# Reading an up-projection's result once: the clamp at minus one on VectorE, and the rest from SBUF

## The chip, the cores and the metric

The kernel runs on one core of a Trainium2 chip. The core has five engines that work side by side, each through its own queue in order: TensorE (PE, with its weight loads listed as PEld), VectorE (DVE), ScalarE (ACT), GpSimd (POOL) and SyncE (SP), which here only issues transfers. Matmul results land in PSUM, which the kernel uses as eight banks of 128 x 512 float32; everything else lies in SBUF. The metric is the device time of one execution in microseconds, and the time of a kernel is the median of its timed runs.

## The reference

Two steps follow each other. The first is an attention without softmax, for 4 batches x 4 heads x 1088 tokens x 32 dimensions, with features that are outer products of two small projections; the second is a feed-forward layer on the 4352 tokens, with a 128 x 2048 matrix up and a 2048 x 128 matrix down:

```
phi(x) = outer(S1 x, S2 x)                    # 8 x 8 = 64 features
kv = sum_s phi(k) v ; z = sum_s phi(k)
x  = (phi(q) kv) / (phi(q) z + 1e-6)
h  = x @ w_in
g  = h                 where h >= 1
     0                 where h <= -1
     (h + 1)^2 / 4     between
out = g @ w_out
```

All inputs come in as float64 and are turned into float32 on the chip. The matmuls of the feed-forward layer run on numbers of a shorter form (fp32r); so that little precision is lost, each operand is split into a high and a low part, and three products are summed (high x high, low x high, high x low).

## The kernel before, in words

**The feed-forward layer** is cut into 144 units: 8 chunks of 512 tokens and one of 256, each with 16 slices of 128 of the 2048 hidden features. The list `units` (L248) gives their order; the first two chunks are woven into each other, and so are the last two. For a unit, `up` (L257) makes three matmuls into one bank, `h` (L262 to L264), and then the curve, whose result g is needed in two parts, `g_hi` and `g_lo = g - g_hi`:

- ScalarE reads the bank, `s = relu(0.5 h + 0.5)` (L270), and squares s in SBUF (L271). So s is ((h+1)/2)^2, and 0 below minus one.
- VectorE computes `min(max(h, 1), s)` from the bank and s. It does so once for g in full precision (L275), and for some 62% of the units a second time, rounded to the short form, for `g_hi` (L274). For the other units ScalarE makes `g_hi` as a cast of g (L277). The function `share` picks them by the fractions in `HI_ACT` (L25): half of the first 32 units, 35% of the rest.
- GpSimd subtracts, `g_lo = g - g_hi`, from SBUF (L278). For the last four units VectorE does it.

`down` (L282) then adds three matmuls into the chunk's accumulator bank, `acc` (L289 to L291). In the program's text it follows its unit by `LAG` = 4 units.

**The attention** is written as generators (`k_steps`, `q_steps`), from which the main loop takes a step after each unit, so that the features of a later batch are computed between units. VectorE has the outer products (L165), the division (L219 to L221) and part of the copies out of PSUM (L207, L235, L236) of that work.

**The weights** of the feed-forward layer are converted by `from_double` in pieces of 512 columns (L82 to L105): VectorE takes the words apart, from and to SBUF (L82, L87, L89, L91, L94), ScalarE has three operations and GpSimd three subtractions, products and sums (L102, L104, L105). Two pieces come before the first unit, the six others between the first units.

**What sets the order:** the program's text is not the order of execution. The context is opened with a scheduler (L412) that places the instructions of each engine by a simulated timeline; on the chip each engine's queue is then worked through in that order, with semaphores between the engines. All PSUM tiles come from one pool of eight banks, and a bank is reused when its last reader is done. SBUF tiles of the curve have rings: five for s and g, six for `g_hi` and `g_lo`.

Of the kernel before, what the change touches and what calls it, by code (L numbers as in the profile page):

```python
# [8 lines left out]
F32 = mybir.dt.float32  # L9
# [4 lines left out]
AF = mybir.ActivationFunctionType  # L14
ALU = mybir.AluOpType
PSUM = bass.MemoryType.PSUM

P = 128
# [2 lines left out]
HI_MAX = 0x47EFFFFF  # L21
HI_MIN = 0x38100000
LAG = 4
FIRST = 32
HI_ACT = (0.5, 0.35)  # L25
FS = "k k k 0f 1f 2f k 0t k 0t 1t 1t K 0n 1n K 0x 2t 2t 1x 2n 2x w"
SS = "0f k k 0t 0t 1f 0n k 1t 0x 1t 2f k 2t 1n 2t 2n 1x k 2x"

# [8 lines left out]
def tile_kernel(ctx: ExitStack, tc: tile.TileContext, qT, kT, v, S, w_in, w_out, outT):  # L37
    nc = tc.nc
# [7 lines left out]
    CH = 512  # L46
# [6 lines left out]
    el = ctx.enter_context(tc.tile_pool(name="el", bufs=3))  # L53
    ps = ctx.enter_context(tc.tile_pool(name="ps", bufs=8, space=PSUM))

    def bank(name):
        return ps.tile([P, 512], F32, tag="ps", name=name)
# [89 lines left out]
    def x_tiles(c0):  # L147
        if c0 not in x_of:
            x_of[c0] = [xs.tile([P, CH], F32R, tag=f"x_{w}", name=f"x_{w}{c0}") for w in ("hi", "lo")]
        return x_of[c0]  # L150
# [97 lines left out]
    units = [*woven(chunks[0], chunks[1], 2), *((c0, n, j) for c0, n in chunks[2:-2] for j in range(NJ)),  # L248
             *woven(chunks[-2], chunks[-1], 3)]

    def share(u, f):
        return int((u + 1) * f) > int(u * f)

    made = {}
    accs = {}

    def up(u):  # L257
        c0, n, j = units[u]
        x_hi, x_lo = x_tiles(c0)
        fj = slice(j * P, (j + 1) * P)  # L260
        h = bank(f"h{u}")
        nc.tensor.matmul(h[:, :n], lhsT=wi_hi[:, fj], rhs=x_hi[:, :n], start=True, stop=False)  # L262
        nc.tensor.matmul(h[:, :n], lhsT=wi_hi[:, fj], rhs=x_lo[:, :n], start=False, stop=False)  # L263
        nc.tensor.matmul(h[:, :n], lhsT=wi_lo[:, fj], rhs=x_hi[:, :n], start=False, stop=True)  # L264

        s = el.tile([P, CH], F32, tag="s", name=f"s{u}", bufs=5)
        g = el.tile([P, CH], F32, tag="g", name=f"g{u}", bufs=5)
        g_hi = el.tile([P, CH], F32R, tag="g_hi", name=f"g_hi{u}", bufs=LAG + 2)
        g_lo = el.tile([P, CH], F32R, tag="g_lo", name=f"g_lo{u}", bufs=LAG + 2)
        nc.scalar.activation(s[:, :n], h[:, :n], AF.Relu, bias=0.5, scale=0.5)  # L270
        nc.scalar.activation(s[:, :n], s[:, :n], AF.Square)  # L271
        by_act = share(u, HI_ACT[u >= FIRST])
        if not by_act:
            nc.vector.scalar_tensor_tensor(out=g_hi[:, :n], in0=h[:, :n], scalar=1.0, in1=s[:, :n], op0=ALU.max, op1=ALU.min)  # L274
        nc.vector.scalar_tensor_tensor(out=g[:, :n], in0=h[:, :n], scalar=1.0, in1=s[:, :n], op0=ALU.max, op1=ALU.min)  # L275
        if by_act:
            nc.scalar.copy(g_hi[:, :n], g[:, :n])  # L277
        (nc.vector if u >= len(units) - 4 else nc.gpsimd).tensor_tensor(  # L278
            out=g_lo[:, :n], in0=g[:, :n], in1=g_hi[:, :n].bitcast(F32), op=ALU.subtract)
        made[u] = (g_hi, g_lo)  # L280
# [63 lines left out]
    for u in range(len(units)):  # L344
        c0, n, j = units[u]
        while todo and todo[0][0] <= j:
            _, src, hi, lo, c, raws, tag = todo.pop(0)
            if c not in raws:
                raws[c] = load_weights(src, c, tag)
            make_weights(raws[c], hi, lo, c)  # L350
        while ready < c0 + n:
            advance()
        first_weights()
        up(u)
        advance()
        if u >= LAG:
            down(u - LAG)
# [58 lines left out]
```

## Time and profile before

| | |
|---|---|
| time, median of 3 runs | 282.25 us (281.66 to 283.06) |
| span of the profiled execution | 423.2 us |
| TensorE clock granted in the profiled execution | 0.555 of full speed |
| busy, PE / DVE / ACT / POOL in the profiled execution | 418.1 / 222.2 / 219.5 / 204.6 us |

The profiled execution is not one of the timed runs, and it lasted half as long again: all through it TensorE was granted little more than half of its clock. The span is the profiled execution's own time from its first to its last instruction; no other time of it is recorded. The durations of the other three engines are their own and do not follow TensorE's clock. So the page has to be read in two parts: how long an operation takes on VectorE, ScalarE and GpSimd can be taken over as it stands, while TensorE's durations, and with them what waits for what, have to be worked out again for a faster clock.

### The profile page before, as it was taken

To read this page: it belongs to the slowest core of one execution; us is meant where nothing else is said; L and a number is where in the kernel's file an instruction comes from. 1 tells how busy PE (TensorE), PEld (TensorE's weight loads), DVE (VectorE), ACT (ScalarE), POOL (GpSimd) and SP (SyncE) were. 2 spreads that over 40 slices of the span, in tenths; PEclk is the share of its full clock that TensorE was granted. 3 is DMA by queue.
4 is the path that set the end of the run, shared out by engine and by line. 5 is a ranking of instruction groups with operands and counts; after the bars stand their busy time and mean duration, and the time that the engine had idled before them with its cause. 6 is when DMAs were issued, how large, how long until landed. Compare 5 with 4: busy or idle time off the path is not lost.

```text
span 423.2 us, 4212 instructions
## 1 busy us (share of the span) xinstructions
PE 418.1 (99%) x1413; PEld 290.9 (69%) x1413; DVE 222.2 (53%) x390; ACT 219.5 (52%) x422; POOL 204.6 (48%) x173
## 2 busy tenths in 40 slices
PE   8999999999999999999999999999999999999997
PEld 6997877778766767786767655555555555567775
DVE  4469966566365453544563463554444444425543
ACT  2336646563354564433544466655566565556662
POOL 0046774747633424333343426646646546435751
PEclk6555555555555555555555555555555555555555
DMA  7942110010000010000000000000000000000001
GB/s 269 415 163 71 52 57 0 2 57 0 0 2 0 0 51 1 1 2 0 0 25 2 0 0 25 2 1 1 25 2 0 0 25 0 2 25 1 2 1 37
DMA packets 4629, 13.90 MB, mean 33 GB/s; under 512 B 512, under 2 KB 1152, under 8 KB 4608
## 3 DMA queue, kind: packets, MB, share of 16 engines
q1 hardware_dynamic: 4608, 13.64, 8.8%
q8 instruction: 11, 0.18, 0.2%
q14 instruction: 10, 0.08, 0.1%
HBM read 11.41 MB, written 2.23 MB: 32 GB/s over the span
## 4 chain that ended last, share of the span: by engine, by line
PE 97%; DMA 1%; DVE 0%; SPq 0%; ACT 0%; issue 0%; ACTq 0%
PE h L264 13%; PE h L262 13%; PE h L263 13%; PE acc L291 12%; PE acc L289 12%; PE acc L290 12%; PE kv L187 6%; PE nd L213 5%; PE tp L206 3%; PE ab_q L160 3%; PE ab_k L160 2%; PE xt L226 2%; DMA q_sb<-in_qT 1%; SPq L113 0%; DVE kp L165 0%; DVE topw L91 0%
## 5 line engine op out<-in xcount | busy, mean ns | idle before, releaser
L278 POOL TENSOR_TENSOR g_lo<-g,g_hi 128x512 fp32r<-128x512 f32 (+1 forms) x140 | 173.1, 1250 | 179.7 <-ACT g_hi L277 108.4
L270 ACT ACTIVATE s<-h 128x512 f32<-128x512 f32 (+1 forms) x144 | 82.3, 574 | 148.9 <-PE h L264 148.2
L274 DVE SCALAR_TENSOR_TENSOR g_hi<-h,s 128x512 fp32r<-128x512 f32 (+1 forms) x89 | 58.0, 651 | 95.5 <-ACT s L271 55.1
L275 DVE SCALAR_TENSOR_TENSOR g<-h,s 128x512 f32<-128x512 f32 (+1 forms) x144 | 92.8, 653 | 27.5 <-ACT s L271 26.7
L271 ACT ACTIVATE s<-s 128x512 f32<-128x512 f32 (+1 forms) x144 | 84.7, 605 | 1.3
L262 PE MATMUL h<-x_hi,wi_hi 128*128 128x512 f32 (+1 forms) x144 | 82.4, 572 | 0.4 <-ACT x_hi L235 0.4
L289 PE MATMUL acc<-g_hi,wo_lo 128*128 128x512 f32 (+1 forms) x144 | 81.4, 566 | 0.0
L264 PE MATMUL h<-x_hi,wi_lo 128*128 128x512 f32 (+1 forms) x144 | 80.6, 560 | 0.0
L291 PE MATMUL acc<-g_lo,wo_hi 128*128 128x512 f32 (+1 forms) x144 | 80.3, 565 | 0.0
L290 PE MATMUL acc<-g_hi,wo_hi 128*128 128x512 f32 (+1 forms) x144 | 79.5, 552 | 0.0
L263 PE MATMUL h<-x_lo,wi_hi 128*128 128x512 f32 (+1 forms) x144 | 79.5, 552 | 0.0
L290 PEld LDWEIGHTS acc<-g_hi,wo_hi 128*128 128x128 f32 x144 | 33.5, 232 | 17.4 <-issue 8.4
L289 PEld LDWEIGHTS acc<-g_hi,wo_lo 128*128 128x128 f32 x144 | 33.3, 231 | 17.3 <-issue 8.6
L291 PEld LDWEIGHTS acc<-g_lo,wo_hi 128*128 128x128 f32 x144 | 33.2, 232 | 16.7 <-issue 8.6
L264 PEld LDWEIGHTS h<-x_hi,wi_lo 128*128 128x128 f32 x144 | 31.2, 216 | 19.6 <-issue 12.0
L262 PEld LDWEIGHTS h<-x_hi,wi_hi 128*128 128x128 f32 x144 | 33.9, 236 | 15.5 <-issue 7.1
L263 PEld LDWEIGHTS h<-x_lo,wi_hi 128*128 128x128 f32 x144 | 32.9, 228 | 16.6 <-issue 10.4
L277 ACT CAST g_hi<-g 128x512 fp32r<-128x512 f32 (+1 forms) x55 | 32.8, 596 | 10.6 <-DVE g L275 10.6
L187 PEld LDWEIGHTS kv<-v_sb,kp 128*128 128x128 f32 x144 | 30.3, 298 | 2.4 <-issue 0.8
L213 PEld LDWEIGHTS nd<-kv_sb,qpT 128*128 128x128 f32 x144 | 29.1, 289 | 3.5 <-issue 1.5
L187 PE MATMUL kv<-v_sb,kp 128*128 128x66 f32 x144 | 29.1, 363 | 0.0
L213 PE MATMUL nd<-kv_sb,qpT 128*128 128x66 f32 x144 | 28.4, 348 | 0.0
(58 smaller groups left out, 267.8 us busy)
## 6 DMA issues: line engine op xcount, KB each, us to landing
v_sb<-in_v SPq DMA_DIRECT2D x4, 594.0 KB, 6.6
q_sb<-in_qT SPq DMA_DIRECT2D x4, 576.0 KB, 7.8
raw_i<-in_w_in SPq DMA_DIRECT2D x4, 512.0 KB, 8.5
raw_o<-in_w_out SPq DMA_DIRECT2D x4, 512.0 KB, 9.7
outT<-o SPq DMA_DIRECT2D x8, 256.0 KB, 2.0
k_sb<-in_kT SPq DMA_DIRECT2D x3, 576.0 KB, 9.3
k_sb<-in_kT SPq DMA_DIRECT2D x3, 192.0 KB, 2.5
outT<-o SPq DMA_DIRECT2D x1, 128.0 KB, 1.9
```

The lines of the kernel that those rows point to most:

```text
L187: nc.tensor.matmul(kv[:, p * VC : (p + 1) * VC], lhsT=kp[:, t, p * P : (p + 1) * P], rhs=v_sb[:, t, p * VC : (p + 1) * VC], start=(t == 0) ...
L213: nc.tensor.matmul(nd[:, c : c + VC], lhsT=qpT[:, p, i * P : (i + 1) * P], rhs=kv_sb[b][:, p].rearrange("p h c -> p (h c)"), start=True, s ...
L262: nc.tensor.matmul(h[:, :n], lhsT=wi_hi[:, fj], rhs=x_hi[:, :n], start=True, stop=False)
L263: nc.tensor.matmul(h[:, :n], lhsT=wi_hi[:, fj], rhs=x_lo[:, :n], start=False, stop=False)
L264: nc.tensor.matmul(h[:, :n], lhsT=wi_lo[:, fj], rhs=x_hi[:, :n], start=False, stop=True)
L270: nc.scalar.activation(s[:, :n], h[:, :n], AF.Relu, bias=0.5, scale=0.5)
L271: nc.scalar.activation(s[:, :n], s[:, :n], AF.Square)
L275: nc.vector.scalar_tensor_tensor(out=g[:, :n], in0=h[:, :n], scalar=1.0, in1=s[:, :n], op0=ALU.max, op1=ALU.min)
L278: (nc.vector if u >= len(units) - 4 else nc.gpsimd).tensor_tensor(out=g_lo[:, :n], in0=g[:, :n], in1=g_hi[:, :n].bitcast(F32), op=ALU.subt ...
L289: nc.tensor.matmul(acc[:, :n], lhsT=wo_lo[:, fj], rhs=g_hi[:, :n], start=(j == 0), stop=False)
L290: nc.tensor.matmul(acc[:, :n], lhsT=wo_hi[:, fj], rhs=g_hi[:, :n], start=False, stop=False)
L291: nc.tensor.matmul(acc[:, :n], lhsT=wo_hi[:, fj], rhs=g_lo[:, :n], start=False, stop=(j == NJ - 1))
```

## The change: what it does

The curve is computed by another chain, with the same value. VectorE clamps h at minus one, from the bank into a new SBUF tile `c` with a ring of four; this is the bank's only reader. ScalarE squares from `c`, with the scale and bias that stood in the Relu before (at c = -1 this gives 0). VectorE takes `min(max(c, 1), s)` with both inputs in SBUF, and the cast to `g_hi` is ScalarE's for every unit. The subtraction for `g_lo` stays where it was. So a unit goes from two ScalarE and one or two VectorE operations, with a third on ScalarE where VectorE has one, to two on each.

```diff
-FIRST = 32
-HI_ACT = (0.5, 0.35)
...
-    def share(u, f):
-        return int((u + 1) * f) > int(u * f)
...
-        nc.scalar.activation(s[:, :n], h[:, :n], AF.Relu, bias=0.5, scale=0.5)
-        nc.scalar.activation(s[:, :n], s[:, :n], AF.Square)
-        by_act = share(u, HI_ACT[u >= FIRST])
-        if not by_act:
-            nc.vector.scalar_tensor_tensor(out=g_hi[:, :n], in0=h[:, :n], scalar=1.0, in1=s[:, :n], op0=ALU.max, op1=ALU.min)
-        nc.vector.scalar_tensor_tensor(out=g[:, :n], in0=h[:, :n], scalar=1.0, in1=s[:, :n], op0=ALU.max, op1=ALU.min)
-        if by_act:
-            nc.scalar.copy(g_hi[:, :n], g[:, :n])
+        c = el.tile([P, CH], F32, tag="c", name=f"c{u}", bufs=4)
+        nc.vector.tensor_scalar(out=c[:, :n], in0=h[:, :n], scalar1=-1.0, scalar2=None, op0=ALU.max)
+        nc.scalar.activation(s[:, :n], c[:, :n], AF.Square, bias=0.5, scale=0.5)
+        nc.vector.scalar_tensor_tensor(out=g[:, :n], in0=c[:, :n], scalar=1.0, in1=s[:, :n], op0=ALU.max, op1=ALU.min)
+        nc.scalar.copy(g_hi[:, :n], g[:, :n])
         (nc.vector if u >= len(units) - 4 else nc.gpsimd).tensor_tensor(
             out=g_lo[:, :n], in0=g[:, :n], in1=g_hi[:, :n].bitcast(F32), op=ALU.subtract)
```

The scheduler makes a new order of it. Line numbers move up by up to eight: in the changed kernel L266 is the clamp, L267 the square, L268 g, L269 the cast and L270 `g_lo`.

**VectorE where the attention's work runs out** (units 78 to 82 of 144; a number behind a tile's name is only its place in the program, and h_2174 before and h_2252 after belong to unit 78). Before:

```order
L274 SCALAR_TENSOR_TENSOR g_hi_2180<-h_2174,s_2178 128x512
L275 SCALAR_TENSOR_TENSOR g_2179<-h_2174,s_2178 128x512
L275 SCALAR_TENSOR_TENSOR g_2195<-h_2190,s_2194 128x512
L274 SCALAR_TENSOR_TENSOR g_hi_2212<-h_2206,s_2210 128x512
L275 SCALAR_TENSOR_TENSOR g_2211<-h_2206,s_2210 128x512
L274 SCALAR_TENSOR_TENSOR g_hi_2228<-h_2222,s_2226 128x512
L275 SCALAR_TENSOR_TENSOR g_2227<-h_2222,s_2226 128x512
L275 SCALAR_TENSOR_TENSOR g_2243<-h_2238,s_2242 128x512
```

and in the changed kernel:

```order
L266 TENSOR_SCALAR c_2260<-h_2252 128x512
L268 SCALAR_TENSOR_TENSOR g_2223<-c_2226,s_2222 128x512
L266 TENSOR_SCALAR c_2277<-h_2269 128x512
L268 SCALAR_TENSOR_TENSOR g_2240<-c_2243,s_2239 128x512
L234 TENSOR_TENSOR x_lo_1936<-xt_2_1929,x_hi_1935 128x256
L266 TENSOR_SCALAR c_2294<-h_2286 128x512
L268 SCALAR_TENSOR_TENSOR g_2257<-c_2260,s_2256 128x512
L266 TENSOR_SCALAR c_2311<-h_2303 128x512
L268 SCALAR_TENSOR_TENSOR g_2274<-c_2277,s_2273 128x512
```

Each unit now has its clamp two units ahead of its g, the two in turn; no row of VectorE reads h and s together any more.

**ScalarE at the same place.** Before, with two rows for each unit and a cast for about one unit in three:

```order
L270 ACTIVATE s_2210<-h_2206 128x512
L277 CAST g_hi_2164<-g_2163 128x512
L270 ACTIVATE s_2226<-h_2222 128x512
L271 ACTIVATE s_2210<-s_2210 128x512
L271 ACTIVATE s_2226<-s_2226 128x512
```

and in the changed kernel:

```order
L267 ACTIVATE s_2256<-c_2260 128x512
L269 CAST g_hi_2224<-g_2223 128x512
L267 ACTIVATE s_2273<-c_2277 128x512
L269 CAST g_hi_2241<-g_2240 128x512
L267 ACTIVATE s_2290<-c_2294 128x512
L269 CAST g_hi_2258<-g_2257 128x512
```

ScalarE no longer reads h; it takes the square of one unit and the cast of the unit two before it in turn.

## The prediction, as it stood before the changed kernel was run

> **What bounds the kernel now.** I read the head of the page first, then the chain that ended last (its last row here is the one long piece of it that isn't TensorE's: start us, us):
>
> ```profile
> PE 418.1 (99%) x1413; PEld 290.9 (69%) x1413; DVE 222.2 (53%) x390; ACT 219.5 (52%) x422; POOL 204.6 (48%) x173
> PEclk6555555555555555555555555555555555555555
> PE 97%; DMA 1%; DVE 0%; SPq 0%; ACT 0%; issue 0%; ACTq 0%
> 2.60 6.00 DMA q_sb<-in_qT
> ```
>
> In the profiled execution TensorE is everything: 97% of the chain, at a granted clock of about 0.555. The timed runs took 282.25 us, against 423.2 us for this execution. Under the same clock that cannot be, since TensorE alone was busy for 418.1 us. At full clock its work would be 418.1 x 0.555 = 232 us, an estimate from these rows, and 282.25 us needs a mean clock of at least 232 / 282 = 0.82. The other engines' durations stay. So in the timed runs VectorE's 222, ScalarE's 220 and GpSimd's 205 us no longer vanish behind TensorE, and I ask stage by stage what is longest. I cut the span at 38 us (first unit's h), 115 us (end of the weight conversion) and 250 us (end of the attention); columns are the stretch, its length, and busy us with counts of PE, PEld, DVE, ACT, POOL:
>
> ```profile
> 0.00:38.00 38.00, 36.06 (x159) 32.01 (x159) 22.55 (x45) 13.32 (x30) 9.14 (x16) 0.56 0.64 240
> 38.00:115.00 77.00, 77.00 (x292) 59.26 (x290) 51.51 (x79) 41.58 (x81) 52.37 (x40) 0.55 0.10 31
> 115.00:250.00 135.00, 135.00 (x476) 95.08 (x476) 67.28 (x126) 64.23 (x117) 50.91 (x40) 0.56 0.02 6
> 250.00:423.00 173.00, 170.06 (x491) 104.57 (x489) 80.88 (x142) 100.39 (x195) 92.23 (x78) 0.56 0.02 9
> ```
>
> With PE's figures times 0.555, the longest engine is, in the second stretch, POOL with 52.4 us (PE 42.7, DVE 51.5); in the third PE with 74.9; in the fourth ACT with 100.4 (PE 94.4, POOL 92.2). The first is a wait for data and then TensorE work at low clock; I put it at 28 us, between 24 (about 9 us until the queries land, and half of the rest) and 38. Sum: 28 + 52.4 + 74.9 + 100.4 = 255.7 us. The time shown is 26.6 us above that floor, for hand-overs and for unevenness within a stretch. So with a fast TensorE no engine rules the whole, and each stretch has two or three within a tenth of each other.
>
> **The change part by part.** Durations by shape:
>
> ```profile
> L278 POOL TENSOR_TENSOR g_lo<-g,g_hi 128x512 fp32r<-128x512 f32 x128 | 164.8, 1299 | 174.6 <-ACT g_hi L277 103.3 <-DVE g L275 43.5 <-PE acc L291 16.0
> L275 DVE SCALAR_TENSOR_TENSOR g<-h,s 128x512 f32<-128x512 f32 x128 | 86.4, 683 | 27.1 <-ACT s L271 26.2 <-POOL g_lo L278 0.7
> L271 ACT ACTIVATE s<-s 128x512 f32<-128x512 f32 x128 | 79.1, 630 | 1.3
> L270 ACT ACTIVATE s<-h 128x512 f32<-128x512 f32 x128 | 76.3, 598 | 142.6 <-PE h L264 142.0
> L278 POOL TENSOR_TENSOR g_lo<-g,g_hi 128x256 fp32r<-128x256 f32 x12 | 8.8, 732 | 5.2 <-ACT g_hi L277 5.2
> L274 DVE SCALAR_TENSOR_TENSOR g_hi<-h,s 128x512 fp32r<-128x512 f32 x77 | 53.0, 688 | 93.8 <-ACT s L271 53.5 <-PE acc L290 27.1 <-ACT g_hi L277 5.4
> L277 ACT CAST g_hi<-g 128x512 fp32r<-128x512 f32 x51 | 31.2, 612 | 10.3 <-DVE g L275 10.3
> L82 DVE TENSOR_SCALAR hcw<-raw_o 128x512 f32<-128x512 f32 x4 | 1.7, 418 | 0.0
> L207 DVE COPY qpT<-tp 128x384 f32<-128x384 f32 x9 | 5.0, 558 | 16.7 <-PE tp L206 16.7
> L235 DVE CAST x_hi<-xt 128x256 fp32r<-128x256 f32 x1 | 0.4, 425 | 2.1 <-PE h L264 2.1
> ```
>
> *ScalarE* loses the Relu (0.60 us a unit) and casts the other 77 large units (0.61): per unit 0.63 + 0.61 = 1.24 us for 0.60 + 0.63 + 0.4 x 0.61 = 1.47. In the fourth stretch, where neighbours overlap by about a tenth (100.4 us of busy time), that is 74 units' worth (66 large, 16 small as half) x 0.23 x 0.9 = 15 us less: 85.
>
> *VectorE* gains a clamp for every unit. No row of before shows it; it is bounded by a one-input read of a bank, 0.558 us at 384 and 0.425 at 256 elements (so 0.69 at 512), and by the two-input 0.68 of L275; I take 0.68. Of it 0.62 counts, since neighbours start about 0.6 us apart (a row of the timeline below has two in 1.27). It loses such a read on 77 large units. The load per unit goes from 0.99 to 1.24 us. That alone is bearable. What the page's averages do not show is the second change: **g now has both inputs in SBUF**. Operations over the whole execution, min/median/max in ns:
>
> ```profile
> L274 DVE SCALAR_TENSOR_TENSOR g_hi<-h,s x89: 411/691/693, 43.1 to 415.8; 128x512 fp32r<-128x512 f32 x77, 128x256 fp32r<-128x256 f32 x12
> L275 DVE SCALAR_TENSOR_TENSOR g<-h,s x144: 412/680/694, 43.7 to 416.2; 128x512 f32<-128x512 f32 x128, 128x256 f32<-128x256 f32 x16
> L89 DVE SCALAR_TENSOR_TENSOR mw<-hcw,mw x8: 679/1086/1655, 13.8 to 101.5; 128x512 int32<-128x512 int32 x8
> L91 DVE SCALAR_TENSOR_TENSOR topw<-topw,mw x8: 674/682/926, 14.7 to 104.2; 128x512 f32<-128x512 f32 x8
> L278 DVE TENSOR_TENSOR g_lo<-g,g_hi x4: 415/416/921, 413.4 to 416.8; 128x256 fp32r<-128x256 f32 x4
> ```
>
> With one input in PSUM, 233 operations never pass 0.694 us whatever GpSimd does. With both in SBUF the same operation takes 0.68 or up to 1.66. The timeline says when:
>
> ```profile
> 43.71 1.27 DVE L275 SCALAR_TENSOR_TENSOR g<-h,s 128x512 f32<-128x512 f32 x2
> 51.77 1.27 POOL L105 TENSOR_TENSOR wo_lo<-topw,loww 128x512 fp32r<-128x512 f32 x1
> 52.65 0.93 DVE L91 SCALAR_TENSOR_TENSOR topw<-topw,mw 128x512 f32<-128x512 f32 x1
> 52.99 3.15 POOL L278 TENSOR_TENSOR g_lo<-g,g_hi 128x512 fp32r<-128x512 f32 x2
> 53.50 1.50 DVE L82 TENSOR_SCALAR hcw<-raw_i 128x512 f32<-128x512 f32 x1
> 104.23 0.68 DVE L91 SCALAR_TENSOR_TENSOR topw<-topw,mw 128x512 f32<-128x512 f32 x1
> 104.53 1.53 POOL L278 TENSOR_TENSOR g_lo<-g,g_hi 128x512 fp32r<-128x512 f32 x1 [1.94 <-ACT g_hi L277]
> 412.80 1.28 POOL L278 TENSOR_TENSOR g_lo<-g,g_hi 128x512 fp32r<-128x512 f32 x1 [0.37 <-ACT g_hi L277]
> 413.44 0.92 DVE L278 TENSOR_TENSOR g_lo<-g,g_hi 128x256 fp32r<-128x256 f32 x1
> ```
>
> L91, the very form of the new g, starts during a GpSimd operation that ends at 53.04 and is itself over at 53.58: 0.54 us later. At 104.23 it came first, ended at 104.91, and GpSimd's subtraction, begun meanwhile, ended at 106.06: 1.15 us later instead of 1.28 after its own start. L82 at 53.50, also from and to SBUF, held up the second of the two subtractions begun at 52.99: it ended at 55.00, the subtraction at 56.14, 1.14 us later. At 413.44 the half-size operation ended 0.28 us after GpSimd's. The two engines take turns. For each large unit the changed kernel has one such g and one such subtraction: **0.54 + 1.14 = 1.68 us in which only one of them moves**, against GpSimd's 1.3 alone before. Busy time and count by stretch: the three rows with two columns are the subtractions (VectorE's last four, then GpSimd's), the next two VectorE's g, the last two its `g_hi`:
>
> ```profile
> 38.00:115.00 77.00, 0.00 (x0) 30.00 (x22) 0.55 0.10 31
> 115.00:250.00 135.00, 0.00 (x0) 50.91 (x40) 0.56 0.02 6
> 250.00:423.00 173.00, 2.08 (x4) 92.23 (x78) 0.56 0.02 9
> 115.00:250.00 135.00, 28.02 (x41) 0.56 0.02 6
> 250.00:423.00 173.00, 49.93 (x81) 0.56 0.02 9
> 115.00:250.00 135.00, 17.14 (x25) 0.56 0.02 6
> 250.00:423.00 173.00, 33.32 (x53) 0.56 0.02 9
> ```
>
> Second stretch: 22 x 1.68 = 37.0; GpSimd's other 18 operations 18 x 1.14 = 20.5; VectorE's weight work from SBUF, six pieces with two operations of two inputs (0.54) and three of one input each, these at 0.28 as an estimate (the half-size hand-over, as the L82 row's 0.42 us is near that operation's 0.415), 11.5. Together 69.0 for 52.4: **+16.6**.
>
> Third: the turns 40 x 1.68 = 67.2; VectorE 67.3 - 25 x 0.62 + 41 x 0.62 = 77.2, beside TensorE's 74.9: **+2.3**. Here VectorE also waits with each g for the rest of a subtraction, and the attention's products and divisions queue behind it, which TensorE awaits. At nothing if something else always fills GpSimd's time, at 41 x (1.14 - 0.62) = 21 us if nothing does; the floor takes nothing, since clamps and attention (67.3 - 28.0 - 17.1 = 22, and 25 us) nearly fill GpSimd's 46.
>
> Fourth: 66 large units x 1.68 = 110.9; 12 small at 0.59 (0.73 less the 0.14 that a hand-over spares) + 0.28 = 0.87, 10.4; the last four, VectorE's own, 4 x (0.41 + 0.42) = 3.3. Together 124.6 for 100.4: **+24.2**. TensorE's 94.4 and ScalarE's 85 lie beside that.
>
> The bank is free after the clamp, 0.7 us after the matmul in place of the 2 to 2.6 of Relu, square and one or two reads. That can only help TensorE run ahead, and what it runs ahead of is the turn-taking: nothing on the floor, up to half of the 26.6 us above it. The chain of a unit is longer by a hand-over, which the order covers: the clamp stands two units ahead of g. Behind a waiting g on VectorE stands the next clamp, for which ScalarE's square waits.
>
> New floor: 28 + 69.0 + 77.2 + 124.6 = 298.8 us. Before, the time lay 26.6 above its floor. I keep nearly all of it (24), because two queues in fixed order lose turns as well: **323 us**. In the profiled execution's own conditions (77, 135 and 173 us for these stretches) the same sums, 69, 77 and 125, fit beneath TensorE, and its 423.2 would stay within 10 us.
>
> On that lock the Trainium skill has a rule (SBUF — State Buffer, "Who interferes with whom"): a VectorE instruction with two SBUF inputs contends with a GpSimd instruction that reads SBUF, and the later one blocks for the whole of the other. By that, 0.68 + 1.30 = 1.98 us a unit, and 128 x 0.30 = 38 us more than my sum; this trace's 0.54 and 1.14 show that part of each duration overlaps, so the sum goes by them.
>
> **The rivals.**
>
> *TensorE is the bound in the timed runs too, at a clock of 0.83.* For it: 28 + 51.4 + 90.2 + 113.7 = 283 us is just the time shown. Against it: the only clocks in this trace are about a half. After the change the stretches would be 69.0, 90.2 and 124.6: 312 us.
>
> *VectorE's queue piles up in the third stretch.* The 21 us above are paid, and again some in the second: above 345, about 350. For it: the products and divisions of the attention queue behind blocked g's. Against it: on average the cover is there.
>
> *No overlap at a hand-over*, the full 1.98 us: 323 + 38 = 361. The five hand-overs above speak against it.
>
> *The other side: faster.* If GpSimd's subtractions mostly find VectorE between its g's, no turn is lost, and what is left is ScalarE's relief, which brings the fourth stretch from 100.4 to between TensorE's 94.4 and VectorE's 80.9 - 53 x 0.62 + 81 x 0.6 = 97, and the early bank: 282 less 3 to 6, less up to half of what lies above the floor, so 263 to 279, say 273. It decides if a g beside GpSimd stays near 0.68 us. Against it: GpSimd works 92 of 100 us in the fourth stretch, so there is no between.
>
> *No change*, 282: TensorE hides all, as in the profiled execution. It would need a clock at which the timed runs are TensorE's (0.83), and a turn in the fourth stretch under 113.7 / 78 = 1.46 us, below the 1.68 of the hand-overs.
>
> **How the numbers follow.** Forecast 0.60, slower TensorE 0.14, pile-up 0.12, no overlap 0.04, faster 0.07, no change 0.03. The measurement of this kernel can tell about 0.5% from no change. Slower: 0.60 + 0.14 + 0.12 + 0.04 = 0.90; same 0.03; faster 0.07. The range goes from just under the bare floor, 296, to the pile-up, 350; outside are the faster and unchanged cases and the worst.
>
> **What would show it.** In the changed kernel's profile, the mean of g at 512 elements near or above 1.0 us with a maximum near 1.8, where now it is 0.683; GpSimd's subtraction above its 1.30; the clamp at 0.68 without spread; and, at a fast TensorE, GpSimd's operations with VectorE's g filling the fourth stretch at about 1.7 us a unit. A g that stays at 0.68 beside a busy GpSimd would prove me wrong, as would a time under 283.

## The result, and the profile after

The changed kernel takes 333.29 us (332.14 to 334.92), the kernel before 282.25 (281.66 to 283.06): 1.178 times as long, with a 95% interval of 1.168 to 1.189. The forecast was 323 us, in a range of 296 to 350. Executions of one kernel differ by up to 3%, so the times below are medians, and the ratios are taken, over the fast runs alone, those within 1.5% of their kernel's fastest, with the kernel before run again beside them.

This time the profiled execution ran at a TensorE clock of 0.953, and its own time, 332.14 us around a span of 330.1, is that of the timed runs. So its rows can be read against the time directly. The head of the page and the chain that ended last:

```profile
PE 293.4 (89%) x1413; PEld 229.1 (69%) x1413; DVE 303.4 (92%) x445; ACT 198.3 (60%) x367; POOL 242.5 (73%) x173
DVE 44%; PE 21%; POOL 13%; issue 13%; ACT 6%; DMA 2%; SPq 1%; DVEq 0%; ACTq 0%; POOLq 0%
DVE g L268 19%; POOL g_lo L270 13%; DVE c L266 11%; PE h L257 3%; PE acc L283 3%; ACT g_hi L269 3%; ACT s L267 2%; DVE kp L163 2%; PE h L259 2%; PE kv L185 2%; PE h L258 2%; DVE mw L85 2%; DMA q_sb<-in_qT 2%; PE acc L281 2%; DVE qp L163 2%
```

VectorE, at 53% in the profile before, is busy for 92%, and the chain goes back and forth between its g and GpSimd's subtraction. GpSimd is busier too (242.5 us for 204.6), although not one of its instructions was changed. The groups by shape, and then two of the lines with min/median/max in ns (these with the sixteen units of half size):

```profile
L270 POOL TENSOR_TENSOR g_lo<-g,g_hi 128x512 fp32r<-128x512 f32 x128 | 194.8, 1545 | 48.8 <-ACT g_hi L269 43.0 <-PE h L259 4.3 <-PE acc L282 1.3
L268 DVE SCALAR_TENSOR_TENSOR g<-c,s 128x512 f32<-128x512 f32 x128 | 139.6, 1101 | 5.5 <-ACT s L267 5.5
L266 DVE TENSOR_SCALAR c<-h 128x512 f32<-128x512 f32 x128 | 85.3, 676 | 1.0 <-PE h L259 1.0
...
L266 DVE TENSOR_SCALAR c<-h x144: 407/677/692, 36.5 to 322.2; 128x512 f32<-128x512 f32 x128, 128x256 f32<-128x256 f32 x16
L268 DVE SCALAR_TENSOR_TENSOR g<-c,s x144: 407/1162/1787, 38.8 to 324.3; 128x512 f32<-128x512 f32 x128, 128x256 f32<-128x256 f32 x16
```

The clamp reads PSUM and has no spread (0.676 us on average, 0.692 at most). The g of two SBUF tensors, of the same sizes and on the same engine, has a median of 1.16 and a maximum of 1.79. The time is in the instructions, not in the gaps between them: VectorE's idle time before its 128 large g's is 5.5 us in all. So VectorE's waits show nothing here; the wait sits inside the busy time. A piece of the timeline in the last stretch shows its shape (VectorE's rows, then GpSimd's, where five subtractions are merged into one row):

```profile
223.69 1.17 DVE L268 SCALAR_TENSOR_TENSOR g<-c,s 128x512 f32<-128x512 f32 x1
224.78 0.68 DVE L266 TENSOR_SCALAR c<-h 128x512 f32<-128x512 f32 x1
225.38 1.16 DVE L268 SCALAR_TENSOR_TENSOR g<-c,s 128x512 f32<-128x512 f32 x1
226.47 0.68 DVE L266 TENSOR_SCALAR c<-h 128x512 f32<-128x512 f32 x1
227.07 1.17 DVE L268 SCALAR_TENSOR_TENSOR g<-c,s 128x512 f32<-128x512 f32 x1
...
220.90 8.49 POOL L270 TENSOR_TENSOR g_lo<-g,g_hi 128x512 fp32r<-128x512 f32 x5
```

VectorE's g's start every 1.69 us (227.07 - 225.38, 225.38 - 223.69), GpSimd's five subtractions take 8.49 / 5 = 1.70 each, and the clamp lies within the time in which g must wait anyway. Over the whole trace, 96 of the 144 g's ran past 0.72 us and ended after a GpSimd operation that had begun before them or shortly after; the median distance between the two ends is 0.55 us, where the prediction took 0.54 from two rows.

For the comparison by stretch, the kernel before was run once more, which gave a profile at a clock of 0.962 (the first experiment below). The cuts are where a unit's result is first read: units 1, 23 and 65, counted from 1, which are the units at which the prediction cut. Columns as in the prediction; before, then after:

```profile
0.00:35.90 35.90, 31.68 (x159) 27.58 (x160) 22.23 (x45) 13.23 (x30) 9.39 (x16) 0.73 0.68 254
35.90:91.00 55.10, 50.64 (x300) 41.94 (x300) 54.26 (x80) 39.74 (x81) 49.63 (x37) 0.99 0.13 43
91.00:173.50 82.50, 82.50 (x472) 70.65 (x471) 64.36 (x120) 61.76 (x118) 54.68 (x44) 1.00 0.03 11
173.50:279.90 106.40, 102.89 (x487) 84.96 (x486) 81.25 (x146) 95.10 (x195) 92.97 (x79) 1.00 0.04 15
```

```profile
0.00:36.50 36.50, 33.15 (x158) 29.27 (x159) 21.94 (x44) 12.90 (x30) 9.03 (x16) 0.92 0.67 250
36.50:106.50 70.00, 59.96 (x314) 46.80 (x314) 69.58 (x97) 37.11 (x70) 55.04 (x38) 0.90 0.11 34
106.50:196.60 90.10, 84.18 (x466) 68.77 (x465) 84.53 (x136) 55.00 (x100) 58.05 (x43) 1.00 0.03 10
196.60:330.10 133.50, 116.08 (x481) 84.23 (x479) 127.40 (x170) 93.30 (x168) 120.39 (x79) 0.96 0.03 12
```

| stretch | before | after | difference | forecast difference of the floors |
|---|---|---|---|---|
| up to the first unit | 35.9 | 36.5 | +0.6 | 0 |
| weight conversion | 55.1 | 70.0 | +14.9 | +16.6 |
| attention | 82.5 | 90.1 | +7.6 | +2.3 |
| the rest | 106.4 | 133.5 | +27.1 | +24.2 |

### The profile page after: what moved, and what is told of

Read it like the earlier page. It is cut to its first block, busy times and chain, and to the rows that moved or that the text cites. A ratio compares the mean times of both kernels' runs of the same rounds, so it can differ in the third digit from the quotient of the medians.

```text
span 330.1 us, 4499 instructions
## 1 busy us (share of the span) xinstructions
PE 293.4 (89%) x1413; PEld 229.1 (69%) x1413; DVE 303.4 (92%) x445; ACT 198.3 (60%) x367; POOL 242.5 (73%) x173
## 4 chain that ended last, share of the span: by engine, by line
DVE 44%; PE 21%; POOL 13%; issue 13%; ACT 6%; DMA 2%; SPq 1%; DVEq 0%; ACTq 0%; POOLq 0%
DVE g L268 19%; POOL g_lo L270 13%; DVE c L266 11%; PE h L257 3%; PE acc L283 3%; ACT g_hi L269 3%; ACT s L267 2%; DVE kp L163 2%; PE h L259 2%; PE kv L185 2%; PE h L258 2%; DVE mw L85 2%; DMA q_sb<-in_qT 2%; PE acc L281 2%; DVE qp L163 2%
## 5 line engine op out<-in xcount | busy, mean ns | idle before, releaser
L270 POOL TENSOR_TENSOR g_lo<-g,g_hi 128x512 fp32r<-128x512 f32 (+1 forms) x140 | 207.3, 1506 | 49.6 <-ACT g_hi L269 43.8
L268 DVE SCALAR_TENSOR_TENSOR g<-c,s 128x512 f32<-128x512 f32 (+1 forms) x144 | 150.7, 1058 | 5.5 <-ACT s L267 5.5
L269 ACT CAST g_hi<-g 128x512 fp32r<-128x512 f32 (+1 forms) x144 | 85.4, 596 | 76.0 <-DVE g L268 57.9
L267 ACT ACTIVATE s<-c 128x512 f32<-128x512 f32 (+1 forms) x144 | 86.8, 608 | 25.1 <-DVE c L266 23.2
L266 DVE TENSOR_SCALAR c<-h 128x512 f32<-128x512 f32 (+1 forms) x144 | 91.4, 647 | 1.0 <-PE h L259 1.0
L281 PE MATMUL acc<-g_hi,wo_lo 128*128 128x512 f32 (+1 forms) x144 | 60.6, 421 | 12.4 <-ACT g_hi L269 12.2
L257 PE MATMUL h<-x_hi,wi_hi 128*128 128x512 f32 (+1 forms) x144 | 59.9, 416 | 0.8 <-DVE c L266 0.4
L282 PE MATMUL acc<-g_hi,wo_hi 128*128 128x512 f32 (+1 forms) x144 | 57.0, 396 | 0.0
L259 PE MATMUL h<-x_hi,wi_lo 128*128 128x512 f32 (+1 forms) x144 | 56.3, 392 | 0.0
L258 PE MATMUL h<-x_lo,wi_hi 128*128 128x512 f32 (+1 forms) x144 | 56.2, 390 | 0.0
```

The source lines that it names most:

```text
L266: nc.vector.tensor_scalar(out=c[:, :n], in0=h[:, :n], scalar1=-1.0, scalar2=None, op0=ALU.max)
L267: nc.scalar.activation(s[:, :n], c[:, :n], AF.Square, bias=0.5, scale=0.5)
L268: nc.vector.scalar_tensor_tensor(out=g[:, :n], in0=c[:, :n], scalar=1.0, in1=s[:, :n], op0=ALU.max, op1=ALU.min)
L281: nc.tensor.matmul(acc[:, :n], lhsT=wo_lo[:, fj], rhs=g_hi[:, :n], start=(j == 0), stop=False)
L282: nc.tensor.matmul(acc[:, :n], lhsT=wo_hi[:, fj], rhs=g_hi[:, :n], start=False, stop=False)
```

## The experiments

**The kernel before, at a full clock.** No edit.

> The kernel before, once more, for a profile at a full TensorE clock like that of the changed kernel (0.953). If the floors of the prediction hold, its stretches (up to the first unit, up to the end of the weight conversion, up to the end of the attention, the rest) are about 28, 58, 87 and 107 us, g reads at 0.68 us and GpSimd's subtraction at 1.30 us, and no engine is busy for much more than 85% of the span. If TensorE was the bound of the timed runs (the rival with a clock of 0.83), it is busy for 97% of the span and the clock is near 0.83.

It took 282.16 us, with a span of 279.9. The head, the chain, GpSimd's large subtractions, and two of TensorE's matmuls six places apart in a dense piece; then two that stand five places apart in the profile of the prediction, at a clock of 0.555:

```profile
PE 267.7 (96%) x1413; PEld 225.1 (80%) x1413; DVE 222.1 (79%) x390; ACT 209.8 (75%) x422; POOL 206.7 (74%) x173
PE 70%; DVE 17%; POOL 5%; issue 3%; DMA 2%; ACT 1%; SPq 1%; POOLq 0%; DVEq 0%; ACTq 0%
L278 POOL TENSOR_TENSOR g_lo<-g,g_hi 128x512 fp32r<-128x512 f32 x128 | 167.4, 1331 | 40.2 <-ACT g_hi L277 18.2 <-DVE g L275 16.3 <-DVE den L220 1.9
223.76 0.39 PE L264 MATMUL h<-x_hi,wi_lo 128*128 128x512 f32 x1
...
225.16 0.39 PE L291 MATMUL acc<-g_lo,wo_hi 128*128 128x512 f32 x1
...
221.53 0.56 PE L264 MATMUL h<-x_hi,wi_lo 128*128 128x512 f32 x1
...
223.45 0.56 PE L289 MATMUL acc<-g_hi,wo_lo 128*128 128x512 f32 x1
```

Neither side is quite right. The clock is full, as the forecast had it and not 0.83. But TensorE is the bound of the last two stretches all the same: 82.5 of 82.5 and 102.9 of 106.4 us. Its matmuls of 512 columns follow each other every (225.16 - 223.76) / 6 = 0.233 us; in the profile of the prediction they stood 0.384 us apart ((223.45 - 221.53) / 5). That is a ratio of 0.61, not 0.555, and 0.61 of the 135 and 170 us of that profile is 82 and 103. In the second stretch VectorE is the bound, with 54.3 of 55.1 us.

**One operand of g back in the bank.** In the program's text this undoes one half of g's move and nothing else of the change; the scheduler then makes a new order of it, as it does for every kernel here:

```diff
-        nc.vector.scalar_tensor_tensor(out=g[:, :n], in0=c[:, :n], scalar=1.0, in1=s[:, :n], op0=ALU.max, op1=ALU.min)
+        nc.vector.scalar_tensor_tensor(out=g[:, :n], in0=h[:, :n], scalar=1.0, in1=s[:, :n], op0=ALU.max, op1=ALU.min)
```

> The changed kernel with one operand of g put back: in0 is h in PSUM in place of c in SBUF. Clamp, square from c, casts on ScalarE and the number and shape of all operations stay; the bank has two readers again and is free some 2 us later. Theory (the two engines take turns because g reads two SBUF inputs): g falls from 1.10 to 0.68 us on average with a maximum below 0.70, GpSimd's subtraction from 1.55 to 1.30, and the time to 283 to 300 us. Rival (the loss is VectorE's extra operation, or the longer chain of a unit): the time stays above 320 us, with g at 0.68 and VectorE idle or waiting in place of it.

It took 287.3 us (1.013 of before, 1.007 to 1.019), 46 us less than the changed kernel for an operand's address.

```profile
L270 POOL TENSOR_TENSOR g_lo<-g,g_hi 128x512 fp32r<-128x512 f32 x128 | 166.6, 1322 | 40.8 <-ACT g_hi L269 31.6 <-PE h L259 6.1 <-PE acc L282 2.7
L266 DVE TENSOR_SCALAR c<-h 128x512 f32<-128x512 f32 x128 | 86.7, 682 | 7.9 <-PE h L259 6.5
L268 DVE SCALAR_TENSOR_TENSOR g<-h,s 128x512 f32<-128x512 f32 x128 | 86.1, 680 | 5.6 <-ACT s L267 5.1
...
L268 DVE SCALAR_TENSOR_TENSOR g<-h,s x144: 412/681/695, 38.9 to 280.2; 128x512 f32<-128x512 f32 x128, 128x256 f32<-128x256 f32 x16
```

g is back at 0.680 us with a maximum of 0.695, and the subtraction at 1.32. Its stretches, cut as above:

```profile
0.00:36.70 36.70, 33.05 (x158) 29.21 (x159) 22.17 (x45) 12.98 (x30) 9.10 (x16) 0.91 0.67 248
36.70:96.60 59.90, 55.95 (x309) 45.86 (x309) 59.56 (x93) 36.29 (x70) 49.74 (x37) 0.94 0.12 40
96.60:179.80 83.20, 82.35 (x467) 69.61 (x466) 74.49 (x141) 54.40 (x101) 55.14 (x44) 1.00 0.03 10
179.80:285.10 105.30, 102.20 (x483) 83.81 (x481) 93.78 (x169) 90.37 (x168) 92.00 (x78) 1.00 0.04 15
```

So the change's loss splits in two. The operations themselves, without the second SBUF input, cost 5.2 us of span: 4.8 in the second stretch, where VectorE was the bound already and now has 59.6 of 59.9 us, and next to nothing in the others, where TensorE has 82.4 of 83.2 and 102.2 of 105.3. The turn-taking is the remaining 45 us of span: 10.1, 6.9 and 28.2 in the three stretches. The rival, that VectorE's extra operation or the longer chain is the loss, is left with a tenth of it. Another rival was not tested by itself: the instructions stand in another order here than in the changed kernel, and the 45 us include what that did. Against it stand the two runs below that end the turns in other ways, each again with an order of its own, at 285.1 and 287.75 us.

**Every second g from the bank.**

```diff
-        nc.vector.scalar_tensor_tensor(out=g[:, :n], in0=c[:, :n], ...
+        nc.vector.scalar_tensor_tensor(out=g[:, :n], in0=(h if u % 2 else c)[:, :n], ...
```

> The changed kernel with g read from the bank for every second unit alone. Theory: half of the turns are gone, so the time lies about half-way between the changed kernel and the one with all g from the bank, 305 to 318 us, and the g of the units that read SBUF keep a mean above 1.0 us while the others are at 0.68. Rival (a threshold: as long as GpSimd keeps up, turns cost nothing): within 3% of the one with all g from the bank.

It took 305.92 us (1.080 of before, 1.072 to 1.088). Both forms of g in one execution:

```profile
L268 DVE SCALAR_TENSOR_TENSOR g<-c,s x72: 408/1182/1787, 39.5 to 297.3; 128x512 f32<-128x512 f32 x58, 128x256 f32<-128x256 f32 x14
L268 DVE SCALAR_TENSOR_TENSOR g<-h,s x72: 407/675/692, 42.7 to 299.1; 128x512 f32<-128x512 f32 x70, 128x256 f32<-128x256 f32 x2
```

The same line of the same program takes 0.68 us or up to 1.79, by the place of one operand. The 58 large g's that read SBUF here cost 305.92 - 287.3 = 18.6 us, the other 70 in the changed kernel 27.4: 0.32 and 0.39 us each. So the rival is out: at half their number the turns are not free. But the stretches differ. Cut as above, this run needs 66.1, 87.1 and 113.6 us, which is 6.2, 3.9 and 8.3 more than with every g from the bank, of the 10.1, 6.9 and 28.2 of all turns. In the last stretch 26 of the 64 large g's read SBUF here, at 0.32 us each, and the other 38 cost 0.52 each in the changed kernel. That the first ones are cheaper there because TensorE needs 102 us of that stretch anyway is likely, but not shown.

**GpSimd writes and doesn't read.** The low part of g is left out of the result; two fills in its place keep GpSimd busy for some 1.1 us a unit (in the last stretch for 71.4 us of 105.0, where the subtractions of the run with g from the bank took 92.0 of 105.3):

```diff
-        (nc.vector if u >= len(units) - 4 else nc.gpsimd).tensor_tensor(
-            out=g_lo[:, :n], in0=g[:, :n], in1=g_hi[:, :n].bitcast(F32), op=ALU.subtract)
+        for _ in range(2):
+            nc.gpsimd.memset(g_lo[:, :n].bitcast(F32), 0.0)
```

> The changed kernel with GpSimd's subtraction left out: g_lo is written as zeros, by two fills a unit, so that GpSimd is still busy for about 1 us a unit but reads nothing, and the low part of g is missing from the result. Theory (what collides is the second SBUF input of g and GpSimd's reading): g is at 0.68 us though GpSimd is busy beside it, and the time is 270 to 295 us. Rival (any GpSimd operation on SBUF collides with it): g stays above 0.9 us on average. Since g_lo no longer hangs on g, a gain beyond that of the bank's operand is due to the shorter chain.

It took 285.1 us (1.008 of before, 0.9995 to 1.016), with g still reading two SBUF tensors. g over the whole execution; then a g beside fills, and one beside GpSimd's part of the weight conversion, which was left in place and reads SBUF:

```profile
L268 DVE SCALAR_TENSOR_TENSOR g<-c,s x144: 412/682/1798, 41.3 to 277.8; 128x512 f32<-128x512 f32 x128, 128x256 f32<-128x256 f32 x16
...
58.80 0.68 DVE L268 SCALAR_TENSOR_TENSOR g<-c,s 128x512 f32<-128x512 f32 x1
58.66 1.11 POOL L271 MEMSET g_lo<- 128x512 f32 x2 [0.29 <-PE acc L283]
...
99.22 1.36 DVE L268 SCALAR_TENSOR_TENSOR g<-c,s 128x512 f32<-128x512 f32 x1
98.75 1.29 POOL L103 TENSOR_TENSOR wo_lo<-topw,loww 128x512 fp32r<-128x512 f32 x1
```

The median is 0.682. Six g's of 144 took over 0.76 us, and each of the six lies beside an operation of the weight conversion on GpSimd. 110 g's lie beside fills alone, and the longest of them took 0.694. So what g collides with is GpSimd's reading. The Trainium skill says the same (SBUF — State Buffer, "Who interferes with whom"): two SBUF inputs on VectorE contend with a GpSimd instruction that reads SBUF and not with one that only writes it; these six agree, and so do the g's beside fills.

**The other operand in the bank.** ScalarE writes the square back into the bank that the clamp has read:

```diff
-        s = el.tile([P, CH], F32, tag="s", name=f"s{u}", bufs=5)
...
-        nc.scalar.activation(s[:, :n], c[:, :n], AF.Square, bias=0.5, scale=0.5)
-        nc.vector.scalar_tensor_tensor(out=g[:, :n], in0=c[:, :n], scalar=1.0, in1=s[:, :n], op0=ALU.max, op1=ALU.min)
+        nc.scalar.activation(h[:, :n], c[:, :n], AF.Square, bias=0.5, scale=0.5)
+        nc.vector.scalar_tensor_tensor(out=g[:, :n], in0=c[:, :n], scalar=1.0, in1=h[:, :n], op0=ALU.max, op1=ALU.min)
```

> The changed kernel with the other operand of g in PSUM: ScalarE writes the square back into the bank that the clamp has read, and g reads c from SBUF and s from the bank. Theory (it is the count of SBUF inputs of g that makes the turns, whichever tensor it is): g at 0.68 us with a maximum below 0.70, and 284 to 292 us, as with h from the bank (287.3). Rival (reading c, fresh from VectorE itself, is what is slow): g stays above 0.9 us and the time above 310 us.

It took 287.75 us (1.019 of before, 1.012 to 1.026), the same as with h from the bank.

```profile
L267 DVE SCALAR_TENSOR_TENSOR g<-c,h 128x512 f32<-128x512 f32 x128 | 86.1, 681 | 6.1 <-ACT h L266 5.5
L266 ACT ACTIVATE h<-c 128x512 f32<-128x512 f32 x128 | 76.7, 602 | 23.7 <-DVE c L265 21.5
```

Reading c is not slow; it is the second input from SBUF that is, whichever it is.

**The casts alone.** From the kernel before, only the third part of the change:

```diff
-        by_act = share(u, HI_ACT[u >= FIRST])
+        by_act = True
```

> The kernel before with one part of the change alone: the high part is cast on ScalarE for every unit; Relu and square stay, so ScalarE has three operations a unit. Theory: ScalarE becomes the bound of the last stretch, with (0.60 + 0.63 + 0.62) x 0.9 = 1.67 us a unit against TensorE's 6 x 0.232 = 1.39, so 74 x 0.28 = 21 us more there and about 300 to 310 us in all, with g at 0.68 us and no turns; the cast for every unit is affordable only with the Relu gone. Rival (casts on ScalarE relieve VectorE, which is the bound of the stretch with the weight conversion): within 1% of before.

It took 301.85 us (1.068 of before, 1.061 to 1.075).

```profile
PE 280.3 (93%) x1413; PEld 230.7 (77%) x1413; DVE 178.5 (59%) x301; ACT 247.2 (82%) x511; POOL 207.0 (69%) x173
L275 DVE SCALAR_TENSOR_TENSOR g<-h,s 128x512 f32<-128x512 f32 x128 | 86.4, 687 | 77.6 <-ACT s L271 77.0 <-issue 0.4
```

VectorE now waits 77 us for ScalarE's square, and g is at 0.687. Of the 20 us, 14 lie in the last stretch (120.4 us from unit 65 on, with ScalarE busy for 116.5, against 106.4), where 21 had been worked out; the mechanism is the one expected, and the price worked out for it was half as much again as the measured one. In the changed kernel the Relu is gone from ScalarE, and its 93 us lie beneath the turns.

**The bank form from unit 65 on.** The kernel before for the first 64 units; then the clamp, the square from SBUF, the cast on ScalarE, and g from the bank:

```diff
-        nc.scalar.activation(s[:, :n], h[:, :n], AF.Relu, bias=0.5, scale=0.5)
-        nc.scalar.activation(s[:, :n], s[:, :n], AF.Square)
-        by_act = share(u, HI_ACT[u >= FIRST])
+        if u < 64:
+            nc.scalar.activation(s[:, :n], h[:, :n], AF.Relu, bias=0.5, scale=0.5)
+            nc.scalar.activation(s[:, :n], s[:, :n], AF.Square)
+        else:
+            c = el.tile([P, CH], F32, tag="c", name=f"c{u}", bufs=4)
+            nc.vector.tensor_scalar(out=c[:, :n], in0=h[:, :n], scalar1=-1.0, scalar2=None, op0=ALU.max)
+            nc.scalar.activation(s[:, :n], c[:, :n], AF.Square, bias=0.5, scale=0.5)
+        by_act = u >= 64 or share(u, HI_ACT[u >= FIRST])
```

> A mixture: the kernel before for the first 64 units, and from there on the clamp, the square from SBUF, the cast on ScalarE, and g from the bank. By the stretches of the runs so far it takes the better of two: 105.3 in place of 106.4 us in the last stretch and before's 4.9 us less in the second, so 281 to 283 us, a gain of 0.4% at most against before. Rival (TensorE's 0.232 us a matmul bounds the last stretch in both, and the difference of 1.1 us is scatter): no difference at all.

It took 284.31 us, 1.005 of before with an interval from 0.9995 to 1.010: no gain, and not the 281 to 283 expected. From unit 65 on it needs 106.3 us, the kernel before 106.4. TensorE bounds that stretch in both (busy for 102.7 and 102.9 us), so the relief of VectorE and ScalarE is worth nothing there. No run of this study beats the kernel before.

## Why the prediction was right, step by step

- **The taking of turns, its cause and its place: right.** Undoing one operand takes 46 of the 51 us away, and g goes from 1.10 to 0.68 us with it. The hand-overs that carried the argument came from a few of VectorE's 390 instructions in the profile before, in the weight conversion and at the very end; what counted is that one of these instructions, L91, was of the new g's form.
- **The size of a turn: right.** 0.54 + 1.14 = 1.68 us were taken from five hand-overs; 1.69 to 1.70 were measured in steady turns. The 1.98 us that full durations give would have been 17% too much.
- **The fourth stretch: +24.2 forecast, +27.1 measured.** The turns took 3% more than worked out. From unit 65 on GpSimd has 76 subtractions, 64 large and 12 small, which ran from 202.0 to 323.4 us, that is 121.4 us; at the prediction's prices they are 64 x 1.68 + 12 x 0.87 = 118.0. Its sum gave 110.9 + 10.4 = 121.3 because its cut in the old profile let in two more; that the two agree is chance. What the sum left out is the run-in and run-out, 5.4 us from the first clamp of the stretch to its first subtraction and 6.7 behind the end of the last one, where the forecast had 3.3.
- **The second: +16.6 forecast, +14.9 measured**, but to a base of 55.1 us instead of 52.4. Its 69.0 us of turns became 70.0, and VectorE is busy for 69.6 of them.
- **The third: +2.3 forecast, +7.6 measured; too small.** The step that failed is "the floor takes nothing": VectorE's wait with each g for the rest of a subtraction had been bounded by 0 and 21 us and set to 0. With g from the bank VectorE is busy for 74.5 us of this stretch, in the changed kernel for 84.5; of these 10 us the turns cost the stretch 6.9.
- **The start: 28 us forecast, 36 to 39 measured.** Too little by 8 or more, and nearly equal before and after (35.9 and 36.5 us), so it moved the sum and not the difference. The 24 us kept "above the floor" had to cover it.
- **What bounded the kernel before: partly wrong.** The prediction scaled TensorE by the clock, 0.555, and got 94.4 us for the last stretch, below ScalarE's 100.4. Scaled by what its matmuls measure, 0.61, it is 103, and TensorE is the bound from unit 23 on. The rival that said so was right in this, at a clock that it didn't need. Its price, 312 us, was too low, because it too took nothing for VectorE's waits and had the same start.
- **The early bank: no gain seen.** With the bank free after the clamp and no turns (fills on GpSimd) the kernel takes 285.1 us; with the bank held until g has been read, 287.3. GpSimd's work differs between the two, so this is no clean measurement, but there is no room for the 13 us that the faster rival had set at most.
- **Not observed:** that the profiled execution's 423.2 us would stay within 10 us under the change. No run of the changed kernel had a clock near 0.555.

The forecast of 323 us was 10 too low. By the stretches: 8.5 in the start, 1.0 in the second, 12.9 in the third (of which TensorE's scale is some 5, since 82.5 and not 74.9 us is its floor there), 8.9 in the fourth and 3.2 beyond the profiled span, together 34.5 above the floor of 298.8, for which 24 had been kept. Those 24 were meant for turns lost by two queues in fixed order; some 14 of the 34.5, the start and TensorE's scale, have nothing to do with that. So the mechanism and the size of a turn were worked out, but that the sum came within 10 us is in part luck. The same two terms make 15.5 of the 26.6 us by which the kernel before stood above its floor (7.9 in the start, 7.6 in the third stretch).

## What to carry to other kernels

Before an operand of a VectorE instruction is moved from PSUM to SBUF, count its SBUF inputs: at two, beside a GpSimd that reads SBUF, the two engines' instructions ran in turns here, and their durations had to be summed (less 0.28 us of 1.98) and no longer compared. The loss shows as a longer duration with a wide spread, not as a wait, so compare min, median and max of one form, and look for a handful of instructions of the new form in the old profile, where the price can be read off beforehand. And where a profile was taken at a low TensorE clock, scale TensorE by the distance of its matmuls in a profile at the clock that matters, not by the clock alone.

## What the runs showed that had not been expected

- TensorE's matmuls of 512 columns follow each other every 0.233 us at a granted clock of 1.00 and every 0.384 at 0.555, where the clock's ratio would have given 0.213 for the first. In a piece of the changed kernel's profile at a clock of 0.50 they stand (285.80 - 284.52) / 3 = 0.427 us apart:

```profile
284.52 0.63 PE L257 MATMUL h<-x_hi,wi_hi 128*128 128x512 f32 x1
...
285.80 0.63 PE L283 MATMUL acc<-g_lo,wo_hi 128*128 128x512 f32 x1
```

0.427 x 0.50 and 0.384 x 0.555 are both 0.213, so between these two clocks the distance follows the clock, and the 0.02 us are added at 1.00 alone; by what, no run shows. They are enough to change which engine is the bound: over the some 390 such matmuls of the last stretch they make 7.8 of the 8.5 us by which it was too short in the prediction (94.4 for 102.9), and over the some 250 of the third 5.0 of its 7.6 (74.9 for 82.5), whose rest stays open.
- At a hand-over the durations of the two engines overlap by 0.28 us in a turn of two: 1.70 us for durations of 0.68 and 1.30. The Trainium skill's rule (SBUF — State Buffer, "Summary: rules for kernel authors"), that the instruction that comes second is blocked until the other has finished, is right in kind and 0.28 us too strict here.
- ScalarE's square takes 0.602 us when it writes to PSUM (row L266 of the run with s in the bank) and 0.63 when it writes to SBUF, with the same input.
